# Attention scores of a banded-attention and gated-MLP kernel computed as 64x64 products instead of 64x128

## The chip, the cores and the metric

The kernel runs on one core of one Trainium2 chip. A core has a matrix engine (TensorE, PE in the profile; its weight loads are shown apart as PEld), a vector engine (DVE), a scalar engine (ACT), GpSimd (POOL) and SyncE (SP), which here only issues DMAs. The engines run their own instruction streams in order and wait for each other through semaphores. Matrix products are written to PSUM, eight banks of 512 fp32 columns in 128 partitions; everything else lives in SBUF.

The metric is the time of one execution on the device in microseconds, the median of the runs taken. Less is better.

## The reference

The input is `q`, `k`, `v` of 8 batches, 8 heads, 576 positions and 64 dimensions, and the weights of a gated layer. Each query sees the 128 keys that end at its own position, with a penalty that grows with the distance:

```python
scores = scale * np.matmul(q, k.transpose(0, 1, 3, 2))
rel = pos[:, None] - pos[None, :]
mask = (rel >= 0) & (rel < 128)
scores = np.where(mask, scores + bias, -1e9)
attn = softmax(scores)
x = np.matmul(attn, v)            # heads side by side: 576 x 512 per batch
h = relu(x @ w_in)                # 576 x 1024, split into u and v
v_n = layer_norm(v)
v_s = w_spatial @ v_n + b_spatial # mixes the 576 positions
out = (u * v_s) @ w_out
```

## The kernel before

Two heads are worked on together as a pair (4 pairs a batch, 32 in all). The 64 dimensions of head 0 lie in partitions 0 to 63 of the tile `raw`, those of head 1 in partitions 64 to 127; `raw[:, 0, :]` holds the queries and `raw[:, 1, :]` the keys, 576 columns each. The 576 queries are cut into five tiles t of 128 (the last has 64). Since a query sees only the 128 keys up to itself, tile t needs the keys from (t-1)·128 to (t+1)·128, which is 256 keys (128 for tile 0, 192 for the last one).

**Scores.** `products` (line 504) multiplies, for each tile and each of the two heads, 64 rows by 128 queries (the stationary operand) by up to 256 keys (the moving one). The two heads use the two halves of the rows of the array and write two PSUM banks. `BANKS` (line 499) says where tiles go: 0 and 1 share a bank of tag `s`, 2 and 3 the next, both with one bank per head, and the last tile goes to the banks of tag `x` from the third batch on. In the second batch (`b < WHOLE`) the last tile is a step of its own, in `s`. There are four `s` banks, two `x` banks and two `m` banks. Then DVE (line 525) reads each 128x256 block from PSUM, adds a table of bias and mask (`tabs`), and writes it to `prob` with the row's extreme value; ACT (line 531) exponentiates it and sums up. Every element of the 128x256 block is read, those outside the band as well; the table puts these at about -2^33.

**Normalising and transposing.** ACT (line 566) and DVE (line 571) split the probabilities into a high and a low fp16 part in `pq`; SP (line 577) transposes `pq` by DMA into `pt`, of which there are three.

**P times V.** `attention` (line 582) splits V into `vh` and `vl` and multiplies 128 keys by 64 columns of V (stationary) by up to 256 queries of `pt` (moving), 42 products a pair (line 633). The two heads use the two halves of the columns of the array. The result takes columns 0 to 287 of the two `x` banks; ACT (line 642) and DVE (line 646) move it into `xt`, and `tail` (line 401) copies a small piece.

**The first five pairs** (batch 0, and the first pair of batch 1) go another way, `raw_tile` (line 420), one tile at a time in fp32: scores at line 434, transposes on TensorE at line 462, P times V at line 480.

**The gated layer.** `gated` works through a batch in 29 units of some 1.6 to 2.8 us on PE, each in one `m` bank: the v half with its layer norm (lines 698 and 720), the u half (line 750), the mixing over positions (line 771) and the output (line 797). `relu` and `copy` (lines 274 and 269) take their results out of PSUM on ACT or DVE.

**What sets the order.** `Plan` collects every step with an engine (or two to choose from), a weight in ns, a due time, and what it reads and writes. `Plan.order` (line 87) then plays the program through with these weights: an engine that is free takes, of the steps whose inputs are there, the one with the earliest due time. The order that comes out is the fixed order of each engine's instructions; on the chip, semaphores keep it right but never change it. `Plan.buf` (line 58) hands out tiles in rotation: the users of the n-th tile of a tag wait for all users of the tile that had the same place before. The last tile's scores and P times V thus take turns in the two places of tag `x`: first the scores of pair p+1 (made when `scores` is called), then P times V of pair p (`AHEAD = 1`).

The due times of a pair, in ns: scores at `due - 5000`, DVE on them from `due - 4500`, the split from `due`, the transposes at `due + 1500` and `due + 3000`, P times V at `due + 5000`. From pair to pair `due` grows by 66000 / 4.

Of the kernel before, what the change touches and what calls it, by code (L numbers as in the profile page):

```python
# [9 lines left out]
F32 = mybir.dt.float32  # L10
# [35 lines left out]
class Plan:  # L46
# [6 lines left out]
    LAG = {"PE": 260, "DVE": 150, "ACT": 170, "POOL": 200, "SP": 2200}  # L53

    def __init__(self):
        self.ops, self.tags = [], {}

    def buf(self, pool, tag, bufs, shape, dtype):
        line = self.tags.setdefault(tag, [])
        before = line[-bufs] if len(line) >= bufs else None  # L60
        line.append(Buf(lambda: pool.tile(shape, dtype, tag=tag, name=tag, bufs=bufs), before, line[-1] if line else None))
        return line[-1]

    def add(self, engine, weight, due, fn, reads=(), writes=()):
# [74 lines left out]
def attn_gmlp_kernel(ctx, tc, qk, v, w_in, w_spT, b_sp, w_out, outT):  # L139
# [3 lines left out]
    nc = tc.nc  # L143
    B, H, D, _, S = qk.shape
    P = 2 * D
# [30 lines left out]
    ctx.enter_context(tc.manual_schedule())  # L176
    plan = Plan()

    def fixed(shape, dtype, name):
        t = const.tile(shape, dtype, name=name)  # L180
        return Buf(lambda: t)
# [46 lines left out]
    def constants():  # L228
        def f():
            nc.gpsimd.iota(relf(), [[-1, 2 * P]], base=P, channel_multiplier=1, allow_small_or_imprecise_dtypes=True)  # L230
        plan.add("POOL", 400, 0, f, (), [(relf, 0)])

        def f():
            nc.vector.memset(maskt(), 0.0)
        plan.add("DVE", dve(256), 0, f, (), [(maskt, 0)])

        def f():
            nc.gpsimd.affine_select(maskt(), maskt(), [[-1, 2 * P]], ALU.is_ge, MASKED, base=P, channel_multiplier=1)
            nc.gpsimd.affine_select(maskt(), maskt(), [[1, 2 * P]], ALU.is_ge, MASKED, base=-1, channel_multiplier=-1)
        plan.add("POOL", 800, 1, f, [(maskt, 0)], [(maskt, 0)])  # L240

        def f():
            nc.vector.memset(ident(), 1.0)
            nc.vector.memset(powers()[:, 0:1], 2.0 ** -12)
            nc.vector.memset(powers()[:, 1:2], 2.0 ** -13 / PSC)
            nc.vector.memset(nhalf(), -0.5)
            nc.vector.memset(rstat(), 1.0)
        plan.add("DVE", dve(400), 500, f, (), [(ident, 0), (powers, 0), (nhalf, 0)] + [(rstat, k) for k in range(8)])

        def f():  # L250
            nc.gpsimd.affine_select(ident(), ident(), [[-1, P]], ALU.is_ge, 0.0, base=0, channel_multiplier=1)
            nc.gpsimd.affine_select(ident(), ident(), [[1, P]], ALU.is_ge, 0.0, base=0, channel_multiplier=-1)
        plan.add("POOL", 600, 500, f, [(ident, 0)], [(ident, 0)])

        def f():
            nc.vector.tensor_scalar(minus(), ident(), -1.0, None, ALU.mult)
        plan.add("DVE", 150, 501, f, [(ident, 0)], [(minus, 0)])
        for j in range(2):
            def f(j=j):
                nc.vector.memset(stat[j](), 1.0)  # L260
            plan.add("DVE", dve(64), 600, f, (), [(stat[j], x) for x in range(99)])
        for h in range(H):
            def f(h=h):
                slope = 2.0 ** (-8.0 * (h + 1) / H)
                nc.vector.scalar_tensor_tensor(tabs[h](), relf(), -8.0 * slope, maskt(), ALU.mult, ALU.add)
            plan.add("DVE", dve(256), 1000 + h * 4000, f, [(relf, 0), (maskt, 0)], [(tabs[h], 0)])
# [153 lines left out]
    def raw_tile(b, p, t, raw, vr, xt, slot, due):  # L420
# [31 lines left out]
        for j in range(2):  # L452
            plan.either([("ACT", act(n, 1), lambda j=j: nc.scalar.activation(pr[j](), pr[j](), AF.Copy, scale=st(RC, j))),
                         ("DVE", dve(n, True), lambda j=j: nc.vector.tensor_scalar(pr[j](), pr[j](), st(RC, j), None, ALU.mult))],
                        due + 1000, cols[j] + [(rstat, row)], cols[j])
        tp = plan.buf(ps, *(("m", 2) if b == 0 else ("s", 4)), [P, 512], F32)

        def f():
            for i, (k, w) in enumerate(blocks):
                for j in range(2):  # L460
                    c = (2 * i + j) * m
                    nc.tensor.transpose(tp()[:w, c:c + m], pr[j]()[:, i * P:i * P + w], ident()[:m, :m])
        plan.add("PE", SWITCH // 2 + pe(*[2 * m] * 2 * len(blocks)), due + 1300, f, cols[0] + cols[1] + [(ident, 0)], [(tp, 0)])
        a0 = (slot // 2) * (NB * P // 2)
        pf = lambda w, x0, x1: pq[slot % 2]().rearrange("p a b -> p (a b)").bitcast(F32)[:w, a0 + x0:a0 + x1]
        pcols = parts(pq[slot % 2], 2 * a0, 2 * (a0 + 4 * P))
        if len({w for _, w in blocks}) == 1:
            e = len(blocks) * 2 * m
            copy(e, lambda: (pf(P, 0, e), tp()[:, :e]), due + 1500, [(tp, 0)], pcols)
        else:  # L470
            for i, (k, w) in enumerate(blocks):
                copy(2 * m, lambda i=i, w=w: (pf(w, 2 * i * m, 2 * (i + 1) * m), tp()[:w, 2 * i * m:2 * (i + 1) * m]), due + 1500,
                     [(tp, 0)], pcols[i::len(blocks)])
        xp = plan.buf(ps, "x", 2, [P, 512], F32)

# [20 lines left out]
                     [k for a in range(2) for k in parts(pq[j], a * NB * P + OFF[NQ - 1], (a + 1) * NB * P)])  # L496


    BANKS = (((0, 1), ("s", 4)), ((2, 3), ("s", 4)), ((4,), ("x", 2)))

    WINDOWS = (((0, 0, 256, 0), (1, 256, 160, 128), (2, 512, 32, 256)),
               ((1, 416, 96, 0), (2, 544, 224, 0), (3, 768, 192, 96), (4, 1024, 64, 224)))
# [1 line left out]
    def products(p, due, st, raw, RAWS, g, banks):  # L504

        SM, NM, RC, TM = range(4)
        sc = [[plan.buf(ps, *tag, [P, 2, 2 * P], F32) for _ in range(2)] for _, tag in banks]
        span = [(k, i, t, min(P, S - t * P), max(0, (t - 1) * P), min(S, (t + 1) * P)) for k, (ts_, _) in enumerate(banks) for i, t in enumerate(ts_)]

        def f():  # L510
            for k, i, t, m, k0, k1 in span:
                for j in range(2):
                    rows = slice(j * D, (j + 1) * D)
                    nc.tensor.matmul(sc[k][j]()[:m, i, :k1 - k0], raw()[rows, 0, t * P:t * P + m], raw()[rows, 1, k0:k1],  # L514
                                     start=True, stop=True)
        plan.add("PE", SWITCH + pe(*[4 * (x[5] - x[4]) for x in span]), due - 5000 + g * 3000, f, RAWS,
                 [(sc[k][j], i) for k, i, *_ in span for j in range(2)])
        for k, i, t, m, k0, k1 in span:
            for j in range(2):
                h, n, c0 = 2 * p + j, k1 - k0, P if t == 0 else 0  # L520
                pt = lambda j=j, m=m, t=t, n=n: prob[j]()[:m, OFF[t]:OFF[t] + n]
                d = due - 4500 + (t if len(banks) < 3 or t < NQ - 1 else -1) * 700 + j * 200

                def f(sc=sc[k][j], pt=pt, i=i, j=j, h=h, t=t, m=m, n=n, c0=c0):
                    nc.vector.tensor_tensor_reduce(pt(), sc()[:m, i, :n], tabs[h]()[:m, c0:c0 + n], -0.125, 3e38,  # L525
                                                   ALU.add, ALU.min, st()[:m, NM, j, t:t + 1])
                cols = parts(prob[j], OFF[t], OFF[t] + n)
                plan.add("DVE", dve(n), d, f, [(sc[k][j], i), (tabs[h], 0)], cols + [(st, (NM, j, t))])

                def f(pt=pt, j=j, t=t, m=m):  # L530
                    nc.scalar.activation(pt(), pt(), AF.Exp, bias=st()[:m, NM, j, t:t + 1], scale=-1.0,  # L531
                                         accum_out=st()[:m, SM, j, t:t + 1])
                plan.add("ACT", act(n, 2), d, f, cols + [(st, (NM, j, t))], cols + [(st, (SM, j, t))])
# [358 lines left out]
```

## Time and profile before

| | us |
|---|---|
| median of 3 runs | 638.37 |
| lowest, highest | 635.79, 638.85 |
| the profiled execution | 636.62 |
| its span, first to last instruction | 634.9 |

The profile is of one execution. It gives the busy time of each engine, the span in 40 slices, the chain of work that ended last, and groups of instructions by line of the kernel. A line such as `PE L514 MATMUL s<-qkraw 64*128 64x256 f32 x324` names the engine, the line of the kernel, the operation, the tile written and the tiles read, for a product the rows and columns of the array that it uses (64*128) and the moving operand (64 partitions by 256 columns), and how many there were; behind the bar stand the busy time, the mean of one in ns and the idle time just before them. Matmuls overlap and their ends are modelled, so a mean of one is longer than the distance from one to the next.

Groups that matter around the change, beside those shown further on:

```profile
L531 ACT ACTIVATE prob<-prob,stat 128x256 f32<-128x256 f32 x162 | 80.3, 499 | 2.0 <-DVE stat L525 2.0
...
L514 PEld LDWEIGHTS s<-qkraw 64*128 64x128 f32 x432 | 36.4, 191 | 8.8 <-issue 4.6 <-DVE stat L525 0.8 <-DVE xt L646 0.5
...
L514 PE MATMUL s<-qkraw 64*128 64x128 f32 x108 | 13.9, 326 | 0.5 <-DVE stat L525 0.5
...
L514 PEld LDWEIGHTS x<-qkraw 64*64 64x64 f32 x96 | 4.7, 131 | 8.0 <-issue 4.0 <-DVE stat L558 1.7 <-DVE gs L271 1.3
```

### The profile page before, as it was taken

Reading aid. Unit: us, or ns where it says so; the run is one execution under the profiler, and the core shown is the slowest. Engines: PE = TensorE matmul, PEld = TensorE weight load, DVE = VectorE, ACT = ScalarE, POOL = GpSimd, SP = SyncE. Lnnn points to the kernel's source line nnn. Section 1 sums busy time; section 2 is a strip of 40 time slices with the busy share of each in tenths; the row PEclk is TensorE's granted clock in tenths of the full one; section 3 lists DMA queues with packets and bytes.
Section 4 is the critical chain, followed back from the end, with each engine's and each line's share of the span. In section 5 each row is a group of like instructions: output and inputs, shape, how many; then the busy total and the mean of one; then the engine's idle time right before and its main releaser. Section 6 shows DMA issues by size and latency. Waiting matters only on the chain.

```text
span 634.9 us, 14049 instructions
## 1 busy us (share of the span) xinstructions
PE 605.2 (95%) x4956; PEld 526.5 (83%) x4956; DVE 538.9 (85%) x1973; ACT 421.0 (66%) x1300; POOL 29.9 (5%) x53
## 2 busy tenths in 40 slices
PE   4879899799899899999999999999999999999997
PEld 2455588688699888999899988998899888998997
DVE  6999898988979899998899899998998899983532
ACT  4698674897856675966497577876596668753211
POOL 1000010000100001000100001000200010000100
PEclk9997799999999999999999999999999999999999
DMA  8903123698845853587555762696558861651001
GB/s 267 336 21 98 49 67 101 149 190 183 174 78 118 190 136 97 115 176 179 116 128 119 197 147 80 121 201 158 119 115 154 166 125 24 112 126 45 1 23 53
DMA packets 153610, 80.22 MB, mean 126 GB/s; under 512 B 132930, under 2 KB 144194, under 8 KB 153540
## 3 DMA queue, kind: packets, MB, share of 16 engines
q1 hardware_dynamic: 153540, 79.32, 53.6%
q8 instruction: 39, 0.64, 0.4%
q14 instruction: 31, 0.25, 0.1%
HBM read 37.13 MB, written 9.44 MB: 73 GB/s over the span
## 4 chain that ended last, share of the span: by engine, by line
PE 62%; DVE 2%; DMA 2%; ACT 1%; issue 0%; ACTq 0%; DVEq 0%
PE m L771 15%; PE m L750 12%; PE m L797 11%; PE m L698 10%; PE s L514 5%; PE x L633 5%; PE m L720 2%; PE x L514 1%; DMA vl<-vl 1%; DMA out_dram<-o 1%; DVE pq L571 1%; DVE xt L646 0%; ACT prob L531 0%; DVE vl L620 0%; DVE o L271 0%
## 5 line engine op out<-in xcount | busy, mean ns | idle before, releaser
L531 ACT ACTIVATE prob<-prob,stat 128x256 f32<-128x256 f32 (+2 forms) x270 | 125.5, 468 | 44.7 <-DVE stat L525 44.7
L771 PE MATMUL m<-wsp,vn 128*128 128x288 f32 x768 | 121.5, 298 | 2.8 <-DVE o L271 2.8
L771 PEld LDWEIGHTS m<-wsp,vn 128*128 128x128 f32 x768 | 107.2, 188 | 6.3 <-DVE o L271 3.4
L750 PE MATMUL m<-xt,win 128*128 128x288 f32 x768 | 111.4, 298 | 0.3 <-ACT u L275 0.3
L797 PE MATMUL m<-gs,wout 128*128 128x288 f32 x768 | 109.6, 298 | 0.1
L566 ACT ACTIVATE pq<-prob,stat 128x128 f16<-128x128 f32 x270 | 104.5, 469 | 5.6 <-ACT prob L531 2.9
L750 PEld LDWEIGHTS m<-xt,win 128*128 128x128 f32 x768 | 104.0, 188 | 4.6 <-issue 1.7
L797 PEld LDWEIGHTS m<-gs,wout 128*128 128x128 f32 x768 | 103.0, 188 | 4.2 <-issue 2.6
L571 DVE SCALAR_TENSOR_TENSOR pq<-prob,stat,pq 128x128 f16<-128x128 f32 x270 | 105.2, 433 | 1.2 <-ACT pq L566 0.7
L698 PE MATMUL m<-win,xt 128*128 128x512 f32 x384 | 92.8, 396 | 2.0 <-DVE vt L729 1.6
L698 PEld LDWEIGHTS m<-win,xt 128*128 128x128 f32 x384 | 72.7, 191 | 19.1 <-issue 2.3
L525 DVE CUSTOM_DVE_ANT_0 prob<-s,tab 128x256 f32<-128x256 f32 (+2 forms) x222 | 75.2, 377 | 0.9
L514 PE MATMUL s<-qkraw 64*128 64x256 f32 (+2 forms) x444 | 52.2, 370 | 3.7 <-DVE stat L525 3.7
L779 DVE TENSOR_TENSOR u<-m,u 128x288 f32<-128x288 f32 x64 | 28.9, 452 | 30.6 <-PE m L771 30.1
L668 POOL TENSOR_TENSOR st<-st,nhalf 128x1 f32<-128x1 f32 (+1 forms) x40 | 25.9, 647 | 548.4 <-DVE st L664 535.5
L531 ACT ACTIVATION_READ_ACCUMULATOR prob<-prob,stat 128x1 f32 (+1 forms) x270 | 51.2, 190 | 0.0
L514 PEld LDWEIGHTS s<-qkraw 64*128 64x128 f32 (+1 forms) x444 | 37.1, 189 | 12.7 <-issue 4.8
L633 PE MATMUL x<-pt,vh 128*64 128x256 f16 (+6 forms) x756 | 41.7, 229 | 0.0
L275 ACT ACTIVATE vt<-m 128x512 f32<-128x512 f32 x32 | 19.1, 596 | 28.6 <-DVE st L663 18.9
L659 DVE BATCH_NORM_STATS2 st<-vt 128x6 f32<-128x512 f32 (+1 forms) x40 | 27.5, 687 | 9.6 <-ACT vt L275 9.6
L633 PEld LDWEIGHTS <-vh 128*64 128x64 f16 x756 | 31.7, 110 | 4.6 <-issue 4.6
L633 PE MATMUL x<-pt,vl 128*64 128x256 f16 (+6 forms) x378 | 35.3, 228 | 0.0
(131 smaller groups left out, 821.2 us busy)
## 6 DMA issues: line engine op xcount, KB each, us to landing
qkraw<-in_qk_dram SPq DMA_DIRECT2D x28, 576.0 KB, 3.8
out_dram<-o SPq DMA_DIRECT2D x64, 144.0 KB, 2.5
vraw<-in_v_dram SPq DMA_DIRECT2D x28, 320.0 KB, 3.2
vn<-in_w_in_dram SPq DMA_DIRECT2D x6, 512.0 KB, 6.7
pt<-in_w_out_dram SPq DMA_DIRECT2D x4, 512.0 KB, 4.6
gs<-in_w_spT_dram SPq DMA_DIRECT2D x4, 288.0 KB, 5.2
xt<-in_w_in_dram SPq DMA_DIRECT2D x2, 512.0 KB, 6.3
qkraw<-in_qk_dram SPq DMA_DIRECT2D x3, 320.0 KB, 8.7
```

What stands on the lines that cost most here:

```text
L514: nc.tensor.matmul(sc[k][j]()[:m, i, :k1 - k0], raw()[rows, 0, t * P:t * P + m], raw()[rows, 1, k0:k1], start=True, stop=True)
L525: nc.vector.tensor_tensor_reduce(pt(), sc()[:m, i, :n], tabs[h]()[:m, c0:c0 + n], -0.125, 3e38, ALU.add, ALU.min, st()[:m, NM, j, t:t + 1])
L531: nc.scalar.activation(pt(), pt(), AF.Exp, bias=st()[:m, NM, j, t:t + 1], scale=-1.0, accum_out=st()[:m, SM, j, t:t + 1])
L566: nc.scalar.activation(pq[j]()[:m, 0, cs], prob[j]()[:m, cs], AF.Copy, scale=st()[:m, RC, j, t:t + 1])
L571: nc.vector.scalar_tensor_tensor(pq[j]()[:m, 1, cs], prob[j]()[:m, cs], st()[:m, RC, j, t:t + 1], pq[j]()[:m, 0, cs], ALU.mult, ALU.subtract)
L633: nc.tensor.matmul(xp()[j * D:(j + 1) * D, x0:x0 + n], l()[:, kt, j * D:(j + 1) * D], rhs[:, o:o + n], start=j not in seen, stop=False, sk ...
L659: nc.vector.bn_stats(st()[:m, 0:6], vt()[:m])
L698: nc.tensor.matmul(pt(), xt[c]()[:, X0[a] + t * P:X0[a] + (t + 1) * P], win()[:, c, w, DH:DF], start=(n == 0), stop=(n == 3 * NC_ - 1))
L750: nc.tensor.matmul(pt()[:, :HS], win()[:, c, w, d * P:(d + 1) * P], xt[c]()[:, X0[a] + hf * HS:X0[a] + (hf + 1) * HS], start=(n == 0), sto ...
L771: nc.tensor.matmul(pt()[:, :HS], l, r, start=(n == 0), stop=(n == len(ops) - 1))
L779: nc.vector.tensor_tensor(u(), pt()[:, :HS], u(), ALU.mult)
L797: nc.tensor.matmul(pt()[:, :HS], wout()[:, d, w, e * P:(e + 1) * P], gs[d]()[:, a, :], start=(n == 0), stop=(n == 3 * ND - 1))
```

## The change

In `products`, each tile of 128 queries is cut into two halves of 64. For the half that begins at query position q, only the keys from q - 128 to q + 64 are multiplied: 192 instead of 256 (in tile 0: 64 for the first half, 128 for the second). The output of a half goes to its own 64 partitions and to the columns of its keys, so that each block keeps its layout. A 128x256 block now has two corners of 64x64 that no product writes: they lie outside the band, but DVE still reads them. So the four `s` tiles are allocated once (`plan.kept`), and DVE clears their second half, the one that nothing else would have written before, at the start.

The last tile's scores move from columns 0 to 191 of the `x` banks to columns 320 to 511 of the same banks, under a tag of their own, `y`. For the planner, `x` and `y` are two rotations that have nothing to do with each other. The planner's weight for the scores follows the narrower products.

```diff
     def buf(self, pool, tag, bufs, shape, dtype):
         line = self.tags.setdefault(tag, [])
         before = line[-bufs] if len(line) >= bufs else None
-        line.append(Buf(lambda: pool.tile(shape, dtype, tag=tag, name=tag, bufs=bufs), before, line[-1] if line else None))
+        kept = self.kept.get(tag)
+        make = (lambda k=len(line) % bufs: kept[k]) if kept else lambda: pool.tile(shape, dtype, tag=tag, name=tag, bufs=bufs)
+        line.append(Buf(make, before, line[-1] if line else None))
         return line[-1]
...
+    plan.kept["s"] = [ps.tile([P, 2, 2 * P], F32, name=f"s{k}") for k in range(4)]
+
+    plan.kept["x"] = [ps.tile([P, 512], F32, name=f"x{k}") for k in range(2)]
+    plan.kept["y"] = [x[:, 512 - 3 * D:].rearrange("p (a b) -> p a b", a=1) for x in plan.kept["x"]]
...
         plan.add("DVE", 150, 501, f, [(ident, 0)], [(minus, 0)])
+        for k in range(4):
+            plan.add("DVE", 340, 100, lambda k=k: nc.vector.memset(plan.kept["s"][k][:, 1, :], 0.0))
...
-    BANKS = (((0, 1), ("s", 4)), ((2, 3), ("s", 4)), ((4,), ("x", 2)))
+    BANKS = (((0, 1), ("s", 4)), ((2, 3), ("s", 4)), ((4,), ("y", 2)))
...
         def f():
             for k, i, t, m, k0, k1 in span:
-                for j in range(2):
-                    rows = slice(j * D, (j + 1) * D)
-                    nc.tensor.matmul(sc[k][j]()[:m, i, :k1 - k0], raw()[rows, 0, t * P:t * P + m], raw()[rows, 1, k0:k1],
-                                     start=True, stop=True)
-        plan.add("PE", SWITCH + pe(*[4 * (x[5] - x[4]) for x in span]), due - 5000 + g * 3000, f, RAWS,
+                for q in range(t * P, t * P + m, D):
+                    for j in range(2):
+                        rows, out = slice(j * D, (j + 1) * D), slice(q - t * P, q - t * P + D)
+                        a, z = max(k0, q - P), q + D
+                        nc.tensor.matmul(sc[k][j]()[out, i, a - k0:z - k0], raw()[rows, 0, q:q + D], raw()[rows, 1, a:z],
+                                         start=True, stop=True, skip_group_check=True)
+        plan.add("PE", SWITCH + pe(*[4 * min(x[5] - x[4], 3 * D) for x in span]), due - 5000 + g * 3000, f, RAWS,
                  [(sc[k][j], i) for k, i, *_ in span for j in range(2)])
```

In `raw_tile`, the tile of the transposes is allocated in the shape of the `s` tiles and seen flattened; its instructions stay the same.

More of the change, by code (lines that the diff above doesn't have):

```diff
@@ L55, in __init__ @@
     def __init__(self):
-        self.ops, self.tags = [], {}
+        self.ops, self.tags, self.kept = [], {}, {}
     def buf(self, pool, tag, bufs, shape, dtype):
@@ L455, in raw_tile @@
                         due + 1000, cols[j] + [(rstat, row)], cols[j])
-        tp = plan.buf(ps, *(("m", 2) if b == 0 else ("s", 4)), [P, 512], F32)
+        tp = plan.buf(ps, *(("m", 2) if b == 0 else ("s", 4)), [P, 2, 2 * P], F32)
+        flat = lambda: tp().rearrange("p a b -> p (a b)")
         def f():
@@ L461, in f @@
                     c = (2 * i + j) * m
-                    nc.tensor.transpose(tp()[:w, c:c + m], pr[j]()[:, i * P:i * P + w], ident()[:m, :m])
+                    nc.tensor.transpose(flat()[:w, c:c + m], pr[j]()[:, i * P:i * P + w], ident()[:m, :m])
         plan.add("PE", SWITCH // 2 + pe(*[2 * m] * 2 * len(blocks)), due + 1300, f, cols[0] + cols[1] + [(ident, 0)], [(tp, 0)])
@@ L468, in raw_tile @@
             e = len(blocks) * 2 * m
-            copy(e, lambda: (pf(P, 0, e), tp()[:, :e]), due + 1500, [(tp, 0)], pcols)
+            copy(e, lambda: (pf(P, 0, e), flat()[:, :e]), due + 1500, [(tp, 0)], pcols)
         else:
             for i, (k, w) in enumerate(blocks):
-                copy(2 * m, lambda i=i, w=w: (pf(w, 2 * i * m, 2 * (i + 1) * m), tp()[:w, 2 * i * m:2 * (i + 1) * m]), due + 1500,
+                copy(2 * m, lambda i=i, w=w: (pf(w, 2 * i * m, 2 * (i + 1) * m), flat()[:w, 2 * i * m:2 * (i + 1) * m]), due + 1500,
                      [(tp, 0)], pcols[i::len(blocks)])
```

## The prediction

> **What bounds the kernel now.** I read the totals first, then the slices, the chain that ended last, and the busy time in stretches of one batch each.
>
> ```profile
> span 634.9 us, 14049 instructions
> PE 605.2 (95%) x4956; PEld 526.5 (83%) x4956; DVE 538.9 (85%) x1973; ACT 421.0 (66%) x1300; POOL 29.9 (5%) x53
> ...
> PEclk9997799999999999999999999999999999999999
> ...
> PE 62%; DVE 2%; DMA 2%; ACT 1%; issue 0%; ACTq 0%; DVEq 0%
> ```
>
> TensorE is busy for 605.2 of 634.9 us, and the chain that ended last, which begins at 209.65 us, lies on TensorE nearly throughout. The clock is granted at 0.9 or more outside two early slices, so times on PE can be compared with each other later on. A total is a mean over stages; the next view takes five stretches of 69.5 us, the time from one batch's layer-norm products to the next batch's.
>
> ```profile
> 162.00:231.50 69.50, 65.67 (x579) 59.21 (x579) 60.81 (x227) 46.92 (x153) 3.30 (x5) 1.00 0.60 136
> ...
> 231.50:301.00 69.50, 69.50 (x610) 62.73 (x609) 64.09 (x237) 49.87 (x159) 3.29 (x5) 1.00 0.63 141
> ...
> sum 347.50, PE 346.96 PEld 313.29 DVE 312.02 ACT 244.46 POOL 16.28; mean PE 69.39 PEld 62.66 DVE 62.40 ACT 48.89 POOL 3.26
> ```
>
> The columns are the stretch, its length, then busy time and count of PE, PEld, DVE, ACT, POOL, then the granted clock. From 231.5 to 579 us PE is busy for 346.96 of 347.5 us; whatever PE time goes there comes off the end, as long as nothing else becomes late. VectorE is next: 64.09 of 69.5 us, 92%. Before 231.5 us PE waits now and then (65.67 of 69.5), so time taken there counts only in part.
>
> **What the scores cost now.** One head pair's scores ("a unit" below) stand in the chain as two pieces:
>
> ```profile
> 244.39 1.72 PE s L514 x16
> 246.11 0.47 PE x L514 x4
> 246.59 3.40 PE m L750 x24
> 249.98 1.51 PE x L633 x42
> 251.49 1.79 PE m L750 x12
> 253.28 1.72 PE s L514 x16
> ```
>
> That is 1.72 + 0.47 = 2.19 us for five tiles and two heads: 10 products, 20 records, so each fp32 product is two records (two rounds). The chain names pieces by their ends and the timeline by starts, which is why the same unit begins at 244.32 below. To split it, I cut narrow windows out of the timeline of PE; each fence line is the start, the time from first start to last end, and the records that touch the window (the ends of matmuls are modelled, so I use starts only).
>
> ```profile
> 244.32 0.37 PE L514 MATMUL s<-qkraw 64*128 64x128 f32 x1
> ...
> 244.65 0.59 PE L514 MATMUL s<-qkraw 64*128 64x256 f32 x3
> ...
> 245.73 0.38 PE L514 MATMUL s<-qkraw 64*128 64x256 f32 x2
> 246.04 0.38 PE L514 MATMUL x<-qkraw 64*64 64x192 f32 x2
> ...
> 246.25 0.33 PE L514 MATMUL x<-qkraw 64*64 64x192 f32 x2
> 246.51 0.41 PE L750 MATMUL m<-xt,win 128*128 128x288 f32 x1
> ```
>
> Tiles 1 to 3 have 256 keys, two rounds each, six rounds; the first starts at 244.65 and the last at 245.73, so a round of 256 keys takes 1.08 / 5 = 0.216 us, for both heads: the two heads run side by side (one after the other they would need twelve). By that rate a round of 192 keys takes 0.162 us and one of 128 keys 0.108 us. Then:
> - tile 0: 0.33 us (244.32 to 244.65), two rounds of 0.108, so 0.11 us of weight load that nothing hides, at the front of the unit;
> - the last six rounds end at 245.73 + 0.216 = 245.95, and the next form starts at 246.04: 0.09 us for the turn from 64x128 to 64x64;
> - last tile: its second round starts 0.21 us after its first, 0.162 of stream and 0.05 of load of the narrower weights; it ends at 246.25 + 0.162 = 246.41, and line 750 starts 0.10 us later, again a turn.
>
> The parts give 0.33 + 1.30 + 0.09 + 0.37 + 0.10 = 2.19.
>
> **The unit after the change.** Tiles 0 to 3 become four products of 64x64 each (two halves of the queries, two heads), the last tile stays two. All are now of the last tile's form, so the turn in the middle goes, and the front load is its 0.05 us. If four run side by side as two do now: 0.05 + 2 x 0.108 (tile 0; its second half still has 128 keys) + 6 x 0.162 (tiles 1 to 3) + 2 x 0.162 (last tile) + 0.10 (the turn out) = **1.66 us, 0.53 less**. If the halves of the array don't keep step, the lower half of tile 0 (64 keys) lets its column run ahead, and the unit could fall to 1.55; I take 1.66, since the rows above show rounds that start in step.
>
> Nothing in the trace runs four fp32 products at once. The nearest rows use either half of the idea. Two heads on two row halves is the round above. Two heads on two column halves is the product P times V:
>
> ```profile
> 107.78 1.09 PE L480 MATMUL x<-pq,vraw 128*64 128x128 f32 x16
> 108.80 0.38 PE L514 MATMUL s<-qkraw 64*128 64x128 f32 x2
> ...
> 250.47 0.21 PE L633 MATMUL x<-pt,vh 128*64 128x32 f16 x4
> 250.53 0.19 PE L633 MATMUL x<-pt,vl 128*64 128x32 f16 x2
> 250.56 0.26 PE L633 MATMUL x<-pt,vh 128*64 128x96 f16 x4
> ```
>
> Line 480, fp32, 16 records of 128 columns with a weight load each, takes 1.02 us to the next product, 0.064 us a record, where a lone round of 128 columns takes 0.108: two columns do run side by side, with different moving data from the same rows and in fp32, loads included. So rows split and columns split each work alone; the value taken is that they work together. The other end is that the column halves run one after the other (a rival below).
>
> The count of records rises from 20 to 36 a unit. Line 633 spends 42 records in 1.51 us, 0.036 us each, and in its 32-column part six matmuls start between 250.47 and 250.56. Eight records a tile at 0.036 are 0.29 us, under the 0.32 us that the tile streams, so issue is not the bound. That is a rival below. The Trainium skill ("TensorE: Matmul & The Clock Gate", section "Wait — 56ns, not 53.3ns?") says that with hardware decode off the sequencer spends about 62 ns on every MATMUL; 36 of them would be 2.23 us, and the unit would gain nothing. The rows of line 633 speak against that here.
>
> **Where the 0.53 us fall.** There are 24 units with the last tile in the x banks (96 records of that form, four each) and three older ones with it apart, in s:
>
> ```profile
> L514 PE MATMUL s<-qkraw 64*128 64x256 f32 x324 | 41.4, 386 | 0.0
> ...
> L514 PE MATMUL x<-qkraw 64*64 64x192 f32 x96 | 13.0, 348 | 0.0
> ```
>
> The 324 records are 27 units of 12. Nineteen of the 24 start between 231.5 and 579 us (four in each of the first four stretches, three in the fifth): 19 x 0.53 = 10.1 us, counted in full. The other five are worth 2.7 us, and the three of the second batch 0.06 (front load) + 6 x 0.054 = 0.38 each, 1.1 us. PE waits there now and then, and a faster unit may only wait longer; I count half of the 3.8: 1.9 us. The scores of the first five head pairs (line 434) are left as they are.
>
> **What else is added or moved.** Four memsets on DVE at the start. A memset of 128x256 in SBUF takes 0.27; none writes PSUM in this trace, and a DVE pass that reads 128x256 there takes 0.41 (line 525), so 1.1 to 1.6 us together, and I take the SBUF row as the same operation.
>
> ```profile
> 1.17 0.27 DVE L234 MEMSET u<- 128x256 f32 x1
> 1.39 0.14 DVE L260 MEMSET stat<- 128x40 f32 x2
> 3.32 0.91 DVE L265 SCALAR_TENSOR_TENSOR tab<-u 128x256 bf16<-128x256 f32 x2 [1.78 <-POOL u L239]
> ...
> 3.24 0.30 POOL L251 TENSOR_SCALAR_AFFINE_SELECT ident<-ident 128x128 f32<-128x128 f32 x1
> ...
> L525 DVE CUSTOM_DVE_ANT_0 prob<-s,tab 128x256 f32<-128x256 f32 x162 | 61.1, 411 | 0.0
> ```
>
> DVE idles 1.78 us there until POOL has made the mask, and that hides either end; POOL comes to ident at 3.24, and DVE, with the memsets ahead, has it written by 3.0. Without that cover they would cost their 1.1 to 1.6 us once. Nothing on SP or POOL is moved by them. That the s tiles are now allocated once, and that the transposes and copies of line 462 on see them flattened, changes no instruction: nothing.
>
> The last tile's scores get other columns of the x banks and leave the planner's rotation of x. Now the order of that rotation puts each P times V (line 633) behind the next unit's last tile and the DVE reads of it. Freed of it, line 633 may come up to 6 us earlier where its transposes have long landed: that of 249.91 had its two issued from 233.45 on.
>
> ```profile
> 233.45 6.12 SPq L577 DMA_TRANSPOSE pt<-pq  x2
> ...
> 248.05 0.34 DVE L525 CUSTOM_DVE_ANT_0 prob<-x,tab 64x192 f32<-64x192 f32 x1
> 248.32 0.34 DVE L525 CUSTOM_DVE_ANT_0 prob<-x,tab 64x192 f32<-64x192 f32 x1
> 249.91 0.41 PE L633 MATMUL x<-pt,vh 128*64 128x256 f16 x4
> ```
>
> With it move two ACT and two DVE evictions, the small copy of tail() and, on SP, the next transposes into the freed pt. PE issues the same work in another order, so I price this at nothing on PE; from both sides it is bounded by the 2.2 us that lie between the end of a unit's scores (246.41) and the end of DVE's reads of its last tile (248.66), gained or waited for. The planner also gets lower weights for the scores (0.32 us a unit by its own formula), so every engine's order shifts a little; taken as nothing, kept in the range as 3 us to each side.
>
> **Does VectorE keep up?** It loses no work. A full stretch shrinks by 4 x 0.53 = 2.1 to 67.4 us, and 64.09 is then 95%. What it waits for now, in the same 347.5 us:
>
> ```profile
> DVE u L779 <- PE m L771: 5.5, 12, 0.6
> DVE prob L525 <- PE x L514: 4.5, 8, 0.9
> ```
>
> 10.0 us are waits for PE, against the 10.1 us that PE gives up: just enough. With nothing left over, some products will wait for an eviction; I take 1 us off.
>
> **Sum.** 10.1 + 1.9 - 1.0 = 11.0 us. The profiled execution took 636.62 us (span 634.9 and 1.7 around it): 625.6. The three runs have their median at 638.37, 1.75 above it, where the same sum gives 627.4. I forecast **626.5**, between the two; alone, this case has 621 to 631 (24 x 0.64 = 15.4 us from a unit of 1.55 at the one end, the order's 3 us against it at the other).
>
> **Rivals.**
> - **VectorE becomes the bound** (0.13). If its waits for PE are latency that a faster PE doesn't shorten, the four full stretches stay at 69.5 us, and what is left is the three units of the last one and the early part: 1.6 + 1.9 = 3.5 us, 633 to 635. For it: 92% now. Against it: the waits are for PE by name, and ACT, with 49.87 of 69.5, can take copies off it.
> - **The column halves take turns** (0.08), the change not doing what it says: tile 0 needs 2 x (0.054 + 0.108), tiles 1 to 3 twelve rounds of 0.162, the unit 0.05 + 0.32 + 1.94 + 0.32 + 0.10 = 2.73, 0.54 more. 24 x 0.54 + 3 x 0.6 is 15 us: **652, slower**. It decides from the point where a tile takes over 0.43 us, two old rounds. Against it: line 480.
> - **A wait in the x banks** (0.05): if writes to a bank still wait for reads of its other columns, and the planner, which sees no such link now, puts line 633 straight behind the scores, PE stands for 2.2 us. Once in each of six batches is 13 us: 638 to 640. The Trainium skill ("PSUM — Partial Sum Buffer", section "PSUM bank collisions raise a hardware error ⚠️") tells to guard by bank and quadrant, not by address, which would keep such waits; no row here shows two engines in one bank. Against it: by the due times P times V comes 6.5 us ahead of the next unit's scores.
> - **Issue becomes the bound** (0.02): it does from 1.66 / 36 = 0.046 us a record on, and at 2.19 / 36 = 0.061 nothing is gained, 637 to 638. Against it: the 0.036 of line 633.
>
> The forecast has 0.72. The range 621 to 635 holds it but for its tails and most of the first rival. About 0.5%, 3 us, is what a measurement of this kernel can tell from no change: faster 0.81 (forecast, and 0.09 of the first rival), within it 0.09 (0.04 of the first, 0.03 of the third, 0.02 of the last), slower 0.10 (the second, and 0.02 of the third, if it waits more than once a batch).
>
> **What would show it.** The unit's pieces in the chain: 1.72 and 0.47 become about 1.2 and 0.4, one piece of 36 records if they are not split, with no 0.09 us ahead of the last tile; tile 1 to 3 rounds start every 0.162 us. If they start every 0.324, the halves take turns. PE's busy share of the stretches stays near 100% and these become 67.4 us; a share of 97% with PE waiting for DVE rows would be the first rival, and a wait of PE on a read of x or y the third. DVE's first tab should stay at 3.32 us. I'd be wrong above all if the fourfold round is not what the two twofold ones suggest.

## The result and the profile after

| | before | after |
|---|---|---|
| median of 8 runs each, taken in turn on one chip, us | 637.25 | 641.76 |
| lowest, highest | 635.79, 638.85 | 640.51, 642.67 |
| ratio, 95% interval | | 1.0077 (1.006 to 1.0094) |
| the profiled execution, us | 636.62 | 641.79 |
| its span, us | 634.9 | 640.1 |

The forecast was 626.5. The kernel became 4.5 us slower instead of some 11 us faster. The lines below are the totals of the changed kernel and its granted clock in 40 slices. Line 527 in it is line 514 before, 538 is 525, 646 is 633, 655 is 642, 659 is 646, 711 is 698, 763 is 750, 784 is 771, 792 is 779, 810 is 797; 281 and 285 are inside `copy` and `relu`.

```profile
span 640.1 us, 14937 instructions
PE 598.2 (93%) x5388; PEld 521.6 (81%) x5388; DVE 533.7 (83%) x1953; ACT 435.0 (68%) x1324; POOL 30.4 (5%) x53
...
PEclk9997799899999999999999999999999999999999
```

PE did 7.0 us less (605.2 before) in a span that is 5.2 us longer, at nearly the same granted clock (0.984 on the mean, 0.987 before). So the products are cheaper, and PE waits. (The 7.0 us don't measure how much cheaper: ends of matmuls are modelled, and the same 768 records of line 810 count 111.5 us now and 109.6 before.) The same stretches as before show where:

```profile
231.50:301.00 69.50, 67.73 (x668) 60.59 (x666) 63.23 (x241) 54.48 (x175) 3.28 (x5) 1.00 0.70 151
301.00:370.50 69.50, 65.89 (x618) 59.93 (x618) 59.24 (x216) 46.25 (x143) 2.94 (x5) 1.00 0.57 129
...
440.00:509.50 69.50, 67.73 (x687) 60.14 (x687) 62.18 (x234) 54.92 (x174) 3.29 (x5) 1.00 0.69 145
...
sum 347.50, PE 334.54 PEld 301.79 DVE 302.88 ACT 251.48 POOL 17.22; mean PE 66.91 PEld 60.36 DVE 60.58 ACT 50.30 POOL 3.44
```

Before, PE was busy for 346.96 of these 347.5 us; now for 334.54. ACT had 159 instructions in each of the first three of these stretches; now it has 175, then 143, and later 174: its work comes in floods. (The batches now take 68.5 to 74.6 us from one layer norm to the next and no longer fit the stretches, so a part of this is only where a stretch begins.) DVE, at 59 to 63 us of 69.5, isn't full either.

**The products did what was forecast.** A unit of five tiles in the chain that ended last, from a part of it near 486 us (start, time, what):

```profile
486.58 1.35 PE s L527 x28
487.94 0.21 PE x L527 x4
488.15 6.88 PE m L810 x48
495.03 1.51 PE x L646 x42
496.54 1.35 PE s L527 x28
497.89 0.24 PE x L527 x4
498.12 0.02 issue
498.15 0.51 ACT xt L655
```

1.35 + 0.21 = 1.56 us in place of 1.72 + 0.47 = 2.19, 0.63 less. (A few of the 36 records are missing here.) Narrow windows of the timeline of PE in another unit, each line the records that touch the window:

```profile
472.45 0.27 PE L527 MATMUL s<-qkraw 64*64 64x64 f32 x2
...
472.62 0.49 PE L527 MATMUL s<-qkraw 64*64 64x192 f32 x8
...
472.78 0.65 PE L527 MATMUL s<-qkraw 64*64 64x192 f32 x9
...
473.06 0.54 PE L527 MATMUL s<-qkraw 64*64 64x192 f32 x8
...
473.11 0.61 PE L527 MATMUL s<-qkraw 64*64 64x192 f32 x8
...
473.38 0.49 PE L527 MATMUL s<-qkraw 64*64 64x192 f32 x6
```

One half of the columns begins rounds of 192 keys at 473.06 and, two later, at 473.38: 0.16 us each. The other half begins at 472.78 and, two later, at 473.11: the same 0.16, some 0.05 us beside the first. So four products run at once, and the column halves keep the same pace without starting together. The first round of 192 comes 0.17 us after the first of tile 0: the half of tile 0 that needs 64 keys lets its column go on.

**The order did not.** Starts on PE of the scores (S) and of P times V (P), read off the trace:

```
before   S244 P250 S253 P268 S273 P282 S291 P296 S314 P319 S323 P337 S342 P351 S360
after    P244 S257 P261 S272 P280 S281 S290 P296 S301 P309 P328 P344 S349 S361 P370
```

Before, S and P take turns throughout. Now three S come within 20 us (281, 290, 301) with one P among them, then no S for 48. The timeline of PE at that place (in brackets the idle time and what ended it):

```profile
290.00 0.77 PE L527 MATMUL s<-qkraw 64*64 64x64 f32 x16
291.08 1.06 PE L527 MATMUL s<-qkraw 64*64 64x192 f32 x13 [0.31 <-DVE stat L538]
...
300.81 0.33 PE L527 MATMUL s<-qkraw 64*64 64x64 f32 x2
302.33 1.54 PE L527 MATMUL s<-qkraw 64*64 64x64 f32 x27 [1.20 <-DVE stat L538]
```

The unit at 301 stands for 1.20 us until DVE has read an earlier unit's scores out of the `s` banks. And ACT, in its timeline at 283 us and at 498 us, has to wait before it can take the result of P times V out of PSUM:

```profile
283.16 0.90 ACT L655 ACTIVATE xt<-x,am 128x288 fp32r<-128x288 f32 x2 [0.85 <-PE x L527]
...
498.15 0.90 ACT L655 ACTIVATE xt<-x,am 128x288 fp32r<-128x288 f32 x2 [0.85 <-PE x L527]
```

In the chain above P times V (line 646) is done at 496.54, but ACT begins to read it at 498.15, when the scores that PE issued after it have put their last tile (line 527, `x`) into other columns of the same bank. ACT has other work until 497.3 and stands for the last 0.85 us. Engines wait for each other through semaphores, and no data goes from the one use to the other: the program guards the bank as a whole. The planner knows of no such link. From 231.5 to 579 us these waits come to (engine, what, for whom: us, times, longest):

```profile
ACT xt L655 <- PE x L527: 5.7, 5, 2.8
...
DVE xt L659 <- ACT xt L655: 3.5, 7, 0.8
```

Before, the first wasn't there, and the second was 3.9 us in 3 waits; so only the first is new (over the whole span it is 8.6 us in 7 waits). What PE itself stands for in the same stretch is in the main ACT:

```profile
PE s L527 <- DVE stat L538: 1.8, 3, 1.2
PE m L763 <- ACT vt L285: 1.8, 2, 1.3
PE m L810 <- DVE u L792: 1.6, 2, 1.1
PE m L711 <- ACT o L281: 1.5, 1, 1.5
PE m L784 <- ACT o L281: 1.5, 2, 0.8
```

The whole list has nine lines and 12.5 us, 9.1 of them for ACT. The theory that I took into the runs: the products gain their 0.63 a unit; the separate `y` loses it and more, through the order. The rivals: the new weight of the scores spoils the order; or DVE was the bound, and the products gain nothing anyway.

### The profile page after: what moved, and what is told of

It reads as the page before. It is cut to its first block, busy times and chain, and to the rows that moved or that the text cites. A ratio compares the mean times of both kernels' runs of the same rounds, so it can differ in the third digit from the quotient of the medians.

```text
span 640.1 us, 14937 instructions
## 1 busy us (share of the span) xinstructions
PE 598.2 (93%) x5388; PEld 521.6 (81%) x5388; DVE 533.7 (83%) x1953; ACT 435.0 (68%) x1324; POOL 30.4 (5%) x53
## 5 line engine op out<-in xcount | busy, mean ns | idle before, releaser
L810 PE MATMUL m<-gs,wout 128*128 128x288 f32 x768 | 111.5, 300 | 4.4 <-DVE u L792 1.6
L711 PE MATMUL m<-win,xt 128*128 128x512 f32 x384 | 94.8, 400 | 3.4 <-ACT vt L285 1.9
L285 ACT ACTIVATE u<-m 128x288 f32<-128x288 f32 x51 | 20.5, 406 | 45.2 <-PE m L763 45.0
L527 PE MATMUL s<-qkraw 64*64 64x192 f32 (+2 forms) x876 | 44.1, 318 | 6.8 <-DVE stat L538 6.8
L527 PEld LDWEIGHTS s<-qkraw 64*64 64x64 f32 x876 | 31.4, 136 | 13.2 <-DVE stat L538 9.7
L281 ACT COPY o<-m 128x288 f32<-128x288 f32 x33 | 13.0, 395 | 33.8 <-PE m L810 32.2
L659 DVE SCALAR_TENSOR_TENSOR xt<-x,am,xt 128x288 fp32r<-128x288 f32 x54 | 25.6, 510 | 12.1 <-ACT xt L655 11.6
```

Of the source, the lines that this page charges most:

```text
L527: nc.tensor.matmul(sc[k][j]()[out, i, a - k0:z - k0], raw()[rows, 0, q:q + D], raw()[rows, 1, a:z], start=True, stop=True, skip_group_chec ...
L659: nc.vector.scalar_tensor_tensor(xt()[:, S + R + hf * HS:S + R + (hf + 1) * HS], xp()[:, :HS], am()[:, 6:7], xt()[:, qs].bitcast(F32), ALU ...
L711: nc.tensor.matmul(pt(), xt[c]()[:, X0[a] + t * P:X0[a] + (t + 1) * P], win()[:, c, w, DH:DF], start=(n == 0), stop=(n == 3 * NC_ - 1))
L810: nc.tensor.matmul(pt()[:, :HS], wout()[:, d, w, e * P:(e + 1) * P], gs[d]()[:, a, :], start=(n == 0), stop=(n == 3 * ND - 1))
```

## The experiments

Each ratio is to the kernel before on the same chip, with its 95% interval; below 1 is faster.

**The parts of the change, one by one.** First the products alone: the last tile stays in the rotation of `x`, the old weight, and memsets that the planner hardly sees, so that every engine keeps the order of before. Against the changed kernel:

```diff
-    plan.kept["x"] = ...
-    plan.kept["y"] = ...
-            plan.add("DVE", 340, 100, ...memset...)
+            plan.add("DVE", 1, 599, ...memset...)
-    BANKS = (..., ((4,), ("y", 2)))
+    BANKS = (..., ((4,), ("x", 2)))
-        plan.add("PE", SWITCH + pe(*[4 * min(x[5] - x[4], 3 * D) for x in span]), ...
+        plan.add("PE", SWITCH + pe(*[4 * (x[5] - x[4]) for x in span]), ...
```

> 64x64 products, but the last tile's scores stay in the rotation of the x banks and the planner keeps the old weight, so each engine has exactly the order of before (plus the four memsets, put at weight 1). Theory A (the order and the bank links that follow from separating x and y cost what the products gained): PE is full in the old order, the unit falls from 2.19 to about 1.56 us, 24 x 0.63 us less of which about 13 us reach the end: 622 to 626 us. Theory B (faster products only make ACT and DVE the bound, whatever the order): at most 3 us gained, 634 to 638 us. Theory C (the products themselves slow something else, memory or clock): 638 us or more.

Then `y` alone, with the products and the weight of before (against before: the two `kept` lines of `x` and `y`, `buf` as in the change, and `("y", 2)` in `BANKS`):

> Old 64x128 products and old weight; only the last tile's scores move to other columns of the x banks, in a rotation of their own. Theory A: the separation alone costs about 16 us, 650 to 656 us. Theory B: no change, 636 to 640 us, since PE is no faster. A middle result (640 to 648) would mean that part of the loss is from the planner's new weight.

The products with the new weight and the change's memsets, the last tile in `x`:

> As e1, but with the new weight of the scores in the planner; x and y stay one rotation. Theory A: close to e1, 622 to 628 us, the difference being what a reshuffle of the order is worth by itself. If the new weight is at fault instead of the separation: near 640 us.

The change with the old weight:

> The changed kernel with the old weight of the scores; PE and ACT have the order of e2. Theory A: 637 to 645 us, like the changed kernel, and about 13 us under e2. If the new weight is at fault: near 625 us.

| kernel | products | last tile | weight | ratio |
|---|---|---|---|---|
| products alone | 64x64 | `x` | old | 0.9984 (0.9966 to 1.0001) |
| `y` alone | 64x128 | `y` | old | 1.0371 (1.0345 to 1.0397) |
| products, new weight | 64x64 | `x` | new | 0.9947 (0.9928 to 0.9966) |
| change, old weight | 64x64 | `y` | old | 1.0189 (1.0156 to 1.0222) |
| change | 64x64 | `y` | new | 1.0077 (1.006 to 1.0094) |

All four medians fell outside what my theory had for them: 635.06 us (622 to 626), 659.57 (650 to 656), 633.17 (622 to 628) and 648.16 (637 to 645). It had the direction of `y` right, and no size.

Two things follow. `y` costs 3.7% with the old products and 2.1% (1.0189 / 0.9984) with the new; the new weight helps in both pairs. And in the order of before, 0.63 us less in each of 24 units, 15 us, bring 1 us, not clear of none at all: the second finding, taken up below. (Every kernel with the new products also has its `s` tiles allocated once; no run has that with the old ones.)

**Which part of `y` costs.** The kernel keeps the change whole, columns too, but for the planner `y` takes its turn in the rotation of `x`:

```diff
-        line = self.tags.setdefault(tag, [])
+        line = self.tags.setdefault("x" if tag == "y" else tag, [])
```

> The changed kernel whole, columns and memsets and weight as changed, except that the planner hands out the last tile's scores and P times V from one rotation again (the engines' order is then exactly that of e3). If the loss lies in the order that the separate rotation lets the planner choose: equal to e3, 632 to 635 us. If it lies in the columns (two uses of one bank, waits between them on the chip): near the changed kernel, 639 us or more.

0.9903 (0.9882 to 0.9925): one line of the planner takes 1.7% back (1.0077 / 0.9903). It was run again beside the products with the new weight, whose traces show the same order on every engine and whose last tile takes its turn in the columns of P times V:

> f1 once more, beside e3 on one chip. If the columns cost nothing and gain nothing: the same as e3 within 2 us. If they help (finer waits): 2 to 4 us under it, as f1 and e3 differed on two chips.

> e3 once more, beside f1: same order of every engine, last tile's scores in a tile of the x rotation. Same as f1 within 2 us, or 2 to 4 us over it, as above.

0.9927 (0.9906 to 0.9947) and 0.997 (0.9953 to 0.9987). Both times the kernel with columns apart was 0.4% ahead of the one with columns shared (0.9903 and 0.9947 on two chips, this pair on one). The two also differ in that the one with columns apart allocates its `x` tiles once and the other takes a new one for each use. Which of the two does it, with one order, stays open. The other columns cost nothing in themselves; the rotation is what paid.

Does it pay because S and P take turns? Two rotations, as in the change, and only a link that makes starts alternate:

```diff
+        group = "x" if tag == "y" else tag
+        last, self.newest[group] = self.newest.get(group), None
...
-        line.append(Buf(make, before, line[-1] if line else None))
+        line.append(Buf(make, before, last))
+        self.newest[group] = line[-1]
```

> The changed kernel with two rotations, and one link between them: P times V of a pair may not start before the next pair's scores have started, nor the scores after that before it. If the bunching of the scores, which this link forbids, is what costs: 631 to 636 us. If it is that the planner doesn't see the waits for reads of the same bank: 638 us or more, since those waits are still unseen.

1.0076 (1.0053 to 1.0099), a miss for the theory: no better than the change. So the turns alone aren't it, as long as the wait on the bank remains. The next two kernels take that wait away with the order as it was: the last tile's products go to free columns of the first `s` bank. The last 64 queries then get other scores, since DVE's pass for the last tile reads tile 1's block. (The edit does a little more than free the bank: each last product of 192 keys becomes one of 128 and one of 64, 96 more records in the run.)

```diff
+                        if len(banks) == 3 and t == NQ - 1:
+                            for c, w in ((a, P), (a + P, D)):
+                                nc.tensor.matmul(sc[0][j]()[out, 0, P:P + w], raw()[rows, 0, q:q + D], raw()[rows, 1, c:c + w], ...)
```

with the order of the change, and with that of alternate starts:

> The changed kernel, every engine in exactly its order, but x and y no longer share a bank: the last tile's products are written to columns of the s banks that tile 0 leaves free (128 and 64 keys, one over the other), and DVE's pass over the last tile reads the first 192 columns of tile 1's block instead. So the last 64 queries of a pair get other scores; every instruction's size stays (two products of 128 and 64 keys stand for one of 192). If the loss is the chip's waits between the two uses of one bank, which the planner no longer sees: 628 to 634 us. If it is the order alone (scores in bunches): 638 us or more, as the changed kernel. Half and half: 634 to 638.

> f2 (scores and P times V alternate, two rotations) with the bank link taken away in the same way as in h1, so that the last 64 queries get other scores; the order is that of f2. If bank waits are what is left of the loss in f2: 627 to 633 us. If the order of f2 is bad in itself: 638 us or more.

| | wait on the bank | none |
|---|---|---|
| order of the change | 1.0077 (1.006 to 1.0094) | 1.0017 (0.9999 to 1.0036) |
| S and P start in turn | 1.0076 (1.0053 to 1.0099) | 0.9973 (0.996 to 0.9987) |
| one rotation | 0.9903 (0.9882 to 0.9925), again 0.9927 | |

The sum over the five stretches of the first of the two without the wait:

```profile
sum 347.50, PE 337.34 PEld 309.58 DVE 301.44 ACT 250.66 POOL 17.20; mean PE 67.47 PEld 61.92 DVE 60.29 ACT 50.13 POOL 3.44
```

PE is busy 2.8 us more than in the change, and its waits for ACT in these stretches fall from 9.1 to 5.4 us; no reader of P times V waits for scores any more. So taking the wait on the bank away is worth 0.6% (3.8 us) in the order of the change and 1.0% in the other. With it gone, taking turns is worth 0.4%. One rotation is another 0.5 to 0.7% ahead, although it keeps both uses in one bank; in its trace, too, no reader of P times V waits for scores. I take the rest for order (a buffer of `x` then also comes free by turns), but no run takes it apart further.

**Why cheaper products bring so little in the order of before.** The sum of the five stretches of the products alone, and its waits from 231.5 to 509.5 us in which PE stood (lines of that kernel: 709 is 698 before, 761 is 750, 782 is 771, 790 is 779, 644 is 633; 279 and 284 are inside `copy` and `relu`):

```profile
sum 347.50, PE 341.06 PEld 311.97 DVE 311.60 ACT 244.83 POOL 16.26; mean PE 68.21 PEld 62.39 DVE 62.32 ACT 48.97 POOL 3.25
```

```profile
PE m L761 <- DVE u L284: 3.1, 4, 0.8
...
PE m L709 <- DVE o L279: 1.1, 2, 0.6
...
PE m L782 <- ACT o L279: 0.5, 1, 0.5
```

PE is at 98% and waits for DVE, once a batch 0.8 us in the u half, at one and the same place. Later its chain leaves PE altogether:

```profile
549.43 0.31 DVE u L790
549.74 6.33 DMA pt<-pq
556.06 0.04 issue
556.11 1.54 PE x L644 x35
```

DVE's split of the probabilities ends late, and P times V waits for the transposes of it. The clock is no rival of weight: it was granted in full (1.00) in all of these stretches, as before; over all runs on that chip it was 0.983 on the mean against 0.987, and the runs of the kernel before differ by some 0.2 us for 0.001. DVE, at 62.3 of 69.5 us, isn't full, but it is late at these places. If DVE is the bound in this sense, then work taken off DVE must help this kernel more than the one before. The low part of V (one DVE instruction a pair) was made for 128 of its 640 columns only, some 14 us of DVE over the run, in both:

```diff
-            nc.vector.scalar_tensor_tensor(vl(), vr(), am()[:, 5:6], vh(), ALU.mult, ALU.subtract)
+            nc.vector.scalar_tensor_tensor(vl()[:, 0], vr()[:, 0], am()[:, 5:6], vh()[:, 0], ALU.mult, ALU.subtract)
```

> The kernel before, with the low part of V made for the first 128 of 640 columns only (the rest of the low part is left out of the computation, as the other columns then hold other numbers): 27 DVE instructions of 0.88 us become about 0.34, 14.4 us less on DVE, about 10 of them between 231 and 579 us; the order stays. If PE alone bounds the kernel before: 633 to 637 us, 2 us less at most. If DVE was near the bound already: under 632 us.

> e1 (64x64 products in the order of before) with the same cut. If DVE has become the bound in e1: 622 to 627 us, 8 us or more under e1 and far more than the cut brings the kernel before. If what holds e1 back is something else (transposes, ACT, the order itself): 632 us or more.

Before with less DVE: 0.993 (0.9911 to 0.9949). Products alone with less DVE: 0.9857 (0.9831 to 0.9883). The sums of their stretches, one fence each:

```profile
sum 347.50, PE 347.45 PEld 314.01 DVE 301.31 ACT 243.45 POOL 13.70; mean PE 69.49 PEld 62.80 DVE 60.26 ACT 48.69 POOL 2.74
```

```profile
sum 347.50, PE 344.71 PEld 315.35 DVE 306.14 ACT 245.77 POOL 14.26; mean PE 68.94 PEld 63.07 DVE 61.23 ACT 49.15 POOL 2.85
```

The time from batch to batch, taken from the starts of the first layer-norm products, from the third batch on: 69.5, 69.5, 69.4 us before; 69.5 each with less DVE, so PE was the bound there. Its 0.7% came from elsewhere, in its profile 1.7 us of it from ahead of the third batch (layer norm at 229.7 us instead of 231.4). With the products alone 69.7, 68.3, 68.4; with less DVE too 67.6, 67.8, 68.1, and PE is at 99%. With DVE relieved the products bring 0.7% (0.9857 / 0.993), not 0.2%. Even so this is a third of what they save: from the third layer norm to the eighth 339.2 us against 345.5, 6.3 of 12 us, and the third begins later (231.4 against 229.7). What holds the rest, no run shows. PE and DVE bound the kernel of before nearly alike: each alone gives little, both together more.

The same cut on top of one rotation:

> f1 with the cut of g1 and g2 (low part of V for 128 of 640 columns only). If DVE still bounds f1: 7 us or more under f1, with batches of about 67.0 us, which PE's own work sets. If f1's order is already bound by PE again: 3 us or less under f1.

0.9856 (0.9829 to 0.9883), 0.5 to 0.7% below one rotation itself. That lies between the two cases that I had expected, and is no more than the cut is worth on the kernel before, so it doesn't show that DVE holds this one.

**What an order is worth.** Three changes of the planner's own numbers, on top of one rotation. Its weight for the scores 180 ns lower:

> f1 with the planner's weight of the scores lowered by another 180 ns to about what the unit takes (1.56 us). If a truer weight helps as the first lowering did between e1 and e3: 627 to 631 us. If such differences are only the luck of the order: 630 to 637 us, either way.

0.9961 (0.9948 to 0.9973), worse than without. Then 300 ns held against DVE wherever a copy may go to ACT or to DVE:

```diff
-                    ends = [max(free[w[0]], now) + queued[w[0]] + w[1] for w in ways]
+                    ends = [max(free[w[0]], now) + queued[w[0]] + w[1] + 300 * (w[0] == "DVE") for w in ways]
```

> f1 with 300 ns added to DVE's end where the planner chooses between ACT and DVE for copies and relus, so that more of them go to ACT. If DVE's load is what keeps f1 from the 67.0 us a batch that PE's work would allow: 625 to 630 us. If ACT then makes DVE wait as much: 631 us or more.

0.9909 (0.9885 to 0.9934), nothing. And the same only for the planner's first 120 us (`300 * (w[0] == "DVE" and now < 120000)`), on one rotation and on the kernel before:

> f1 with the 300 ns of f4 only in the planner's first 120 us. In f4 the first two batches ended 6 us sooner than in f1 and the later ones took 69.5 instead of 67.8 us. If both can be had: 624 to 628 us. If the early gain is lost again to the DVE chain: 630 to 633 us.

> The kernel before with f5's 300 ns in the planner's first 120 us, old products and one rotation. If f5's step under f6 (11 us) is the early copies alone, it does as much here: 625 to 628 us, and the products are worth 5 us in f5. If it needs the new products (the steady batches stay at 69.5 us here): 630 to 633 us.

0.9753 (0.9729 to 0.9778), a median of **620.74 us**, faster than both kernels of this study; and 0.9885 (0.985 to 0.992), 630.74 us, for the early copies on the kernel before. So of the 2.5%, some 1.2% are the early copies and 1.3% (0.9753 / 0.9885) the products with an order that suits them. The totals of the faster one, and a stretch of the first two batches in it and then before:

```profile
span 618.7 us, 14921 instructions
PE 590.0 (95%) x5388; PEld 519.6 (84%) x5388; DVE 536.1 (87%) x1959; ACT 426.7 (69%) x1318; POOL 30.9 (5%) x53
```

```profile
36.00:112.00 76.00, 70.10 (x529) 52.03 (x528) 69.96 (x254) 62.27 (x185) 5.58 (x7) 0.96 0.26 82
```

```profile
36.00:112.00 76.00, 69.38 (x471) 51.64 (x472) 69.21 (x244) 55.36 (x159) 4.46 (x7) 0.91 0.22 70
```

In the same 76 us ACT does 185 instructions in place of 159, DVE 254 in place of 244 and PE 529 records in place of 471 (some of those because the products have more records). The granted clock there was 0.96 in place of 0.91; how much of the early gain is that, and whether it follows from the order, no run tells apart.

## Why the prediction was wrong

- **The unit after the change: right, at the upper end of the saving.** Taken was 1.66 us, and 1.55 named for the case that the column halves don't keep step. They don't, and it is 1.56: the tile 0 term was 0.1 us too dear. Turns of the column halves (rival two, 2.73 us) and issue (rival four) are out. Its 36 records take 1.56 / 36 = 0.043 us each. The Trainium skill ("TensorE: Matmul & The Clock Gate", section "Wait — 56ns, not 53.3ns?") has some 62 ns for a MATMUL with hardware decode off. The 0.043 of this trace speak against that bound here.
- **The memsets: right.** DVE's first `tab` still starts at 3.32 us.
- **The step that failed first: the order.** The prediction said of the separate `y` that "PE issues the same work in another order, so I price this at nothing on PE", bounded by 2.2 us, and of the weight "every engine's order shifts a little; taken as nothing, kept in the range as 3 us to each side". The order with `y` in a rotation of its own, and the waits on the bank that come with it, cost 1.5 to 1.7% against one rotation, some 10 us; with the products of before `y` costs 3.7%, 24 us. The sharing of one rotation looked like a hindrance to P times V, which "may come up to 6 us earlier". It was also the pace: never two S without a P between them. That the planner, freed of it, would bunch the scores and that the engines behind would be flooded and then idle was not among the rivals.
- **The third rival, half right.** It had PE standing for reads of the same bank. The wait came the other way round: the reader of P times V (ACT 655, then DVE 659) waited for a product that PE issued later into other columns. The 0.6% of the table are the price of it here. The longest of these waits was 2.8 us, near the 2.2 a time that the rival had. The Trainium skill ("PSUM — Partial Sum Buffer", section "PSUM bank collisions raise a hardware error ⚠️") tells to guard a bank, not an address, and not writes alone. By these waits the program does so; what an unguarded read would do, no run shows.
- **The other step that failed: PE's savings counted in full.** "Does VectorE keep up" had "10.0 us are waits for PE, against the 10.1 us that PE gives up: just enough. With nothing left over, some products will wait for an eviction; I take 1 us off." In the very order of before, the products alone gave 1 us (0.9984) of a predicted 11; the loss through `y` hid this. Of the 10.0 us of DVE's waits for PE, 5.2 are left there from 231.5 to 579 us, while PE already stands for DVE: some half of them could be given away, the rest not, as rival one feared with its 0.13. That the products alone came to 635.06, next to the 633 to 635 of rival one, is in part luck, since the kernel before had 635.52 on that chip; the rival had 3.5 us off. Nor did the stretches stay at 69.5, as it said: they took 69.7, 68.3 and 68.4. In its profile the five batches from the third layer norm to the eighth took 343.8 us instead of 346.4: 2.6 of the 12 us that their 19 units gave up. The early part, for which I counted 1.9 us, gave none: the third batch's layer norm started at 231.7 us there, at 231.4 before. Its granted clock was lower in that part (0.93 against 0.97 from 112 to 162 us, 0.98 against 1.00 from there to 231.5); how much of the 1.9 this took, no run tells.
- **The range** of 621 to 635 left out every case in which the order itself costs more than 3 us. For a planner that plays the whole program through, that bound came from no row.

## What to carry to other kernels

A buffer that two steps share may be what sets their pace. When a change unties them, keep the old order (one rotation) and free only the storage; here this was the step from 1.0077 to 0.990. Saved time on an engine that is 100% busy counts only as far as the next one, at 92%, can follow without its own waits; take work off both at once. And where two uses share a PSUM bank, give the planner the bank as one thing where the program guards it as one: here the readers of one use waited for the writes of the other.

## What the runs showed of the hardware

Four fp32 products of 64x64 with 192 columns run side by side, and each half of the columns takes its next round after 0.16 us whether or not the other is in step; five tiles of two heads take 1.56 us where products of 64x128 take 2.19. A reader of one set of columns of a PSUM bank waited up to 2.8 us for a product into other columns, with no data shared; this is a wait of the program's semaphores, and no run leaves it out with both uses in the bank. And two kernels with one order of instructions, apart in which columns of two banks the last tile's scores take and in how often the tiles in these banks are allocated, differed by 0.4% in two pairs of runs (0.9903 and 0.9947, 0.9927 and 0.997); the cause is open.
